# An attention kernel fused with a two-layer softplus network: wide matmuls in the second half of the first layer, and one written order for all steps

## The chip, the cores and the metric

The program runs on one core of a Trainium2 chip. The metric is device time in microseconds (us), lower is better. Before the change three runs took 216.32, 216.36 and 217.01 us, a median of 216.36 us.

## The reference

```python
scores = scale * np.matmul(q, k.transpose(0, 1, 3, 2))      # batch 4, 8 heads, 768 tokens, head size 64
is_global = pos[None, :] < n_global                          # the first 8 tokens of a batch
is_local = (rel >= 0) & (rel < n_local)                      # the last 96 tokens
scores = np.where(is_global | is_local, scores + bias, -1e9) # bias: -slope(head) * distance
a = softmax(scores)
x = matmul(a, v)                                             # as 3072 tokens x 512
h = x @ w_in                                                 # 512 -> 2048
g = np.maximum(h, 0.0) + np.log1p(np.exp(-np.abs(h)))        # softplus
out = g @ w_out                                              # 2048 -> 512
```

Inputs and output are float32. The kernel computes in bfloat16 with float32 sums.

## The kernel before

The 3072 tokens are 24 blocks n of 128; six blocks make one batch of the attention. A block attends to itself, to the block before it, and to the 8 global tokens, which are copied into unused places of the previous block's keys and values. For the two layers the tokens are 12 chunks of 256.

The work is cut into named steps, and each step issues its instructions on several engines. Every engine has its own queue and takes its instructions in the order in which the program writes them; it waits at each for the semaphores that this one needs. The steps:

- `lq lk lv` with a block number: load a block of q, k or v from HBM, with a cast to bfloat16. POOL issues it (line 99). `wi`, `wo`: a quarter of w_in or w_out (lines 105, 110).
- `g` with a number: POOL reads one element of a result of the first layer (line 475), so that what stands behind it in POOL's queue starts no sooner. The numbers are those of `f`.
- `t` (blocks 1 to 7): transpose q and k of a block on the PE and copy them out on DVE, to QT and KT. `d` (from block 8): the same by two DMA transposes that SP issues (lines 251 and 252). `tq tk cq ck` do block 0.
- `s n`: scores. From block 6 on the step s n.0 holds both halves of the heads: matmuls of 64 rows into s_ps, and into s_lo and the bank `o2` for the second half; DVE adds the bias into Z (lines 314, 316, 339). For blocks 0 to 3 the bias comes from matmuls (`z`).
- `e n.half`: exponential on ACT (line 348), four heads.
- `p n.half`: probabilities times v on the PE into x_ps (line 363), one PSUM bank, then on DVE a reciprocal (line 374) and the multiplication into xsf (line 377). xsf is a ring of two blocks, so p of block n writes where block n - 2 lay.
- `x` (blocks 0 to 3, 5) and `y` (all others): transpose xsf into XT, on the PE and DVE, or by one DMA transpose that SP issues (line 388).
- `f`: first layer, 96 steps. A step takes two of the 16 feature blocks of one chunk: for each, four matmuls (512 inputs in four parts) of 256 columns into half of an hT bank (line 416). ACT then does exp and ln(x + 1) on 512 columns (lines 421, 422) into G. hT has two banks.
- `o`: second layer, 96 steps, eight for a chunk: four matmuls of 512 columns (line 438). After four steps a group of 128 tokens is complete; DVE copies it out (line 444) and SP stores it. The banks are `o` and `o2`; from block 6 on until chunk 9 only `o`, since the scores take `o2`. In the last chunk the steps o92 to o95 (line 460) do the last 128 tokens in two parts: o92 and o93 give 320 columns in the bank `o2`, o94 and o95 give 192 columns in the bank `o`.

The first part of the order is written out by hand (ORDER); the rest is sorted by due times: f u at u + 0.5, o u at u + 9.9, attention of block n around 4n - 12.4. The last steps before the change are therefore f95 o86 o87 o88 o89 o90 o91 o92 o93 o94 o95. Gates and loads follow the same times.

Of the kernel before, what the change touches and what calls it, by code (L numbers as in the profile page):

```python
# [19 lines left out]
def kernel(  # L20
# [19 lines left out]
    CT = 2 * P  # L40
# [41 lines left out]
    w_out_c = [const.tile([P, NFB // NWC, DM], BF16, name=f"w_out{c}") for c in range(NWC)]  # L82
# [7 lines left out]
        for n in range(lo, hi):  # L90
            nc.vector.memset(v_t[n][:, :, D : D + 1], 1.0)

    warm_in = const.tile([P, CT], BF16, name="warm_in")
    nc.vector.memset(warm_in[:], 0.0)
    ones(0, 2)

# [24 lines left out]
    def load_v(n):  # L121
# [5 lines left out]
            name=nc.get_next_instruction_name(),  # L127
# [81 lines left out]

    def fill(dst):  # L210

        for _ in range(fillers[0]):
            nc.tensor.matmul(dst, warm_in[:, 0:P], warm_in[:, 0 : dst.shape[1]])
        fillers[0] = 0

    def wide(t):
        return t.rearrange("p a b -> p (a b)")[:, 0:CT]

    def first_of(n):
        return n - n % BPB  # L220

    def qk_bank():
        if fillers[0]:
            fill(ps.tile([P, CT], F32, tag="tr", name="tr_w")[:])
        return ps.tile([P, 2, NPAIR, P], BF16, tag="tr", name="tr")

    def tr_in(tr, j, src):
# [153 lines left out]

    def tr_x(n, by_dma=False):
        xsf, _ = xt.pop(n)
        if n % 2 == 0:
            XT[n // 2] = xtp.tile([P, NPAIR, CT], BF16, tag="XT", name="XT")
        dst = XT[n // 2][:, :, P * (n % 2) : P * (n % 2) + P]
        if by_dma:
            nc.sync.dma_start_transpose(dst, xsf[:].rearrange("p h d -> p (h d)"))
            return
        if n < 2:  # L390
            fillers[0] = 0
            tr = ps2.tile([P, 2, NPAIR, P], BF16, tag="hT", name="tr_x")
# [11 lines left out]
        u = max(u for u in W_IN if 2 * u <= fb)  # L404
        return w_in_c[u], (fb - 2 * u) * P

    def ffn1(c, u):
        if c not in G:
            G[c] = ffn.tile([P, NFB, CT], BF16, tag="G", name="G")
        hT = ps2.tile([P, 2, CT], F32, tag="hT", name="hT")  # L410
        fill(hT[:, 0, :])
        for j in range(2):
            fb = 2 * u + j
            w, fo = w_in_of(fb)
            for m in range(KM):
                nc.tensor.matmul(  # L416
                    hT[:, j, :], w[:, m, fo : fo + P], XT[c][:, m, :],
                    start=(m == 0), stop=(m == KM - 1),
                )
        e_sb = work.tile([P, 2, CT], F32, tag="e_sb", name="e_sb")  # L420
        nc.scalar.activation(e_sb[:], hT[:], AF.Exp)  # L421
        nc.scalar.activation(G[c][:, 2 * u : 2 * u + 2, :], e_sb[:], AF.Ln, bias=1.0)  # L422

    def o_bank(i):
        return o_tile(i, [P, DM])
# [1 line left out]
    def ffn2(c, u):  # L427
        if c == NCH - 1 and u >= NWC:
            ffn2_last(u)
            return  # L430
        ns, kq = divmod(u, NWC)
        if kq == 0:
            O[c, ns] = o_bank(ns if c == 0 or c >= NCH - 3 else 0)
            fill(O[c, ns][:, 0:CT])
        fillers[0] = 0
        o = O[c, ns]
        for a in range(NFB // NWC):
            nc.tensor.matmul(  # L438
                o[:], G[c][:, 4 * kq + a, ns * P : ns * P + P], w_out_c[kq][:, a, :],
                start=(kq == 0 and a == 0), stop=(kq == NWC - 1 and a == 3),  # L440
            )
        if kq == NWC - 1:
            osb = work.tile([P, DM], F32, tag="osb", name="osb")
            nc.vector.tensor_copy(osb[:], O.pop((c, ns))[:])  # L444
            n0 = c * CT + ns * P
            nc.sync.dma_start(out[n0 : n0 + P, :], osb[:])
# [3 lines left out]
    def ffn2_last(u):  # L450

        c, ns = NCH - 1, 1
        c0, w, bank = (0, LW, 1) if u < 6 else (LW, DM - LW, 0)
        fbs = range(NU * (u % 2), NU * (u % 2) + NU)
        if fbs[0] == 0:
            O["last"] = o_bank(bank)
        o = O["last"]
        for fb in fbs:
            kq, a = divmod(fb, NFB // NWC)
            nc.tensor.matmul(  # L460
                o[:, 0:w], G[c][:, fb, ns * P : ns * P + P], w_out_c[kq][:, a, c0 : c0 + w],
                start=(fb == 0), stop=(fb == NFB - 1),
            )
# [7 lines left out]

    def gate(s):

        c, u = divmod(s, NU)
        nc.gpsimd.tensor_copy(gate_t[:], G[c][0:1, 2 * u + 1, 0:1])  # L475

    LAG = 9

    ORDER = """
        w16 lq1 z0.1 lk1 b0 cq0 ck0 tq0 tk0 z0.0 s0.0 e0.0 s0.1 t1 lv0 e0.1 z1.0 b1 z1.1 s1.0 lq2 lk2 lv1  # L480
        s1.1 p0.0 e1.0 e1.1 gk2 lq3 p0.1 t2 p1.0 x0 bb0 lk3 lv2 z2.0 p1.1 gv2 lv3 z2.1 s2.0 s2.1 wi0 wi2 t3
        gk3 e2.0 p2.0 z3.0 s3.0 e2.1 p2.1 lq4 gv3 z3.1 x1 e3.0 s3.1 e3.1 lk4 bb1 p3.0 gk4 x2 lq5 p3.1 f0 x3
        wo0 lk5 gv4 f1 f8 wi4 f2 t4 f9 s4.0 lv4 f10 wo1 wi6 lv5 f11 wo2 s4.1 o4 e4.0 wo3 t5 f3 g11 o0 e4.1
        lq6 gk5 s5.0 f4 p4.0 f12 f5 s5.1 f13 e5.0 o5 o1 lk6 f6 p4.1 f7 gv5 y4 e5.1 lq7 f14 p5.0 f15 o2 p5.1
        lk7 lv6 o6 x5 g7 o3 o7 lk8 t6 lq8 o8 lk9 f16 s6.0 e6.0 f17 f18 t7 p6.0 lv7 g13 lq9 e6.1 f19 s7.0 g15
        lv8 o9 d8 g19 o10 p6.1 gk8 lk10 d9 lq10 y6 o11 e7.0 lk11 f20 g17 e7.1 f21 p7.0 o12 f22 p7.1 s8.0
        e8.0 w2 gv8 o13 o14 y7 o15 e8.1 f23 gk9 p8.0 lv9 s9.0 e9.0 d10 o16 p8.1 e9.1 lq11 d11 gv9 o17 o18
        f24 g23 lk12 p9.0 f25 g21 gk10 y8 f26 p9.1 o19 f27 s10.0 o20 lv10 gk12 lq12 e10.0 f28 y9 o21 gv10
        o22 g27 e10.1 p10.0 g25 f29 gk11 f30 d12 o23 s11.0 lk13 f31 o24 p10.1 lv11 e11.0 lq13 gv11 e11.1 o25
        f32 f33 d13 p11.0 s12.0 e12.0 y10 f34 o26 p11.1 g29 y11 f35 gv12 g31 lk14 lv12 o27 f36 f37 e12.1 o28  # L490
        f38 s13.0 lq14 o29 f39 e13.0 g35 gk14 d14 o30 f40 f41 g33 lk15 lv13 lq15 p12.0 o31 e13.1 g37 f42
        p12.1 g39 lv14 o32 d15 f43 p13.0 s14.0 y12 lq16 g41 lv15 f44 p13.1 g43 lk16 e14.0 o33 y13 gv13 d16
        o34 lk17 gv14 lq17 gk13
    """

    def steady(n):

        s = 4 * n - 12.4
        return {
            f"d{n}": s - 8.2, f"gv{n}": s - 0.95, f"gk{n}": s - 0.9, f"s{n}.0": s,  # L500
            f"e{n}.0": s + 0.7, f"e{n}.1": s + 1.7, f"p{n}.0": s + 1.95, f"p{n}.1": s + 2.95,
            f"y{n}": s + 3.25,
        }

    fillers = [0]

# [28 lines left out]
    def run(name):  # L535
        kind = name.rstrip("0123456789.")
        nums = [int(i) for i in name[len(kind):].split(".")]
        if kind in "fo":
            (ffn1 if kind == "f" else ffn2)(*divmod(nums[0], NU))
        else:  # L540
            KINDS[kind](*nums)

    first_steps = ORDER.split()
    for name in first_steps:
        run(name)
    todo = {}
    for n in range(RV, NB):
        todo.update(steady(n))
    for n in range(RV, NB):
        for names, u in ((f"lq{n}", f"lk{n}"), 4 * n - 25), ((f"lv{n}",), 4 * n - 19):  # L550
            todo[f"g{u}"] = u + 1.6
            for i, name in enumerate(names):
                todo[name] = u + 1.7 + 0.01 * i
    for u in range(NU * NCH):
        todo[f"f{u}"] = u + 0.5
        todo[f"o{u}"] = u + LAG + 0.9
    for name in sorted(todo.keys() - set(first_steps), key=lambda x: (todo[x], x)):
        run(name)


# [33 lines left out]
```

## Time and profile before

The profiled execution took 217.16 us by the device's clock; its span from the first to the last instruction is 215.4 us, so 1.8 us lie around the span. The granted TensorE clock was 1.000 in it.

| engine | busy, us | share of the span | instructions |
|---|---|---|---|
| PE (matmul) | 207.0 | 96% | 2004 |
| PEld (weight load) | 143.5 | 67% | 2004 |
| ACT | 161.4 | 75% | 255 |
| DVE | 109.0 | 51% | 261 |
| POOL | 73.8 | 34% | 115 |

| DMA issued by | what | count | median us from issue to landing |
|---|---|---|---|
| POOL | q, k, v blocks | 70 | 4.6 to 5.1 |
| POOL | w_in, w_out quarters | 8 | 11.6, 13.3 |
| SP | QT, KT, XT transposes | 51 | 4.5 to 4.6 |
| SP | results | 25 | 3.5 (256 KB) |

A matmul's row in the profile lasts until its last result is there; matmuls overlap, so the mean duration of one (273 ns with 256 columns) is longer than the distance at which they follow each other. In the chain of waits a piece "x16" is sixteen matmuls in a row, and its length divided by sixteen is that distance. A name such as `XT<-xsf` says what an instruction writes and reads. SPq and POOLq are the queues that issue DMAs; the bracket at the end of a timeline row tells how long the engine sat idle before it and what ended that.

### The profile page before, as it was taken

Reading aid. Unit: us, or ns where it says so; the run is one execution under the profiler, and the core shown is the slowest. Engines: PE = TensorE matmul, PEld = TensorE weight load, DVE = VectorE, ACT = ScalarE, POOL = GpSimd, SP = SyncE. Lnnn points to the kernel's source line nnn. Section 1 sums busy time; section 2 is a strip of 40 time slices with the busy share of each in tenths; the row PEclk is TensorE's granted clock in tenths of the full one; section 3 lists DMA queues with packets and bytes.
Section 4 is the critical chain, followed back from the end, with each engine's and each line's share of the span. In section 5 each row is a group of like instructions: output and inputs, shape, how many; then the busy total and the mean of one; then the engine's idle time right before and its main releaser. Section 6 shows DMA issues by size and latency. Waiting matters only on the chain.

```text
span 215.4 us, 5027 instructions
## 1 busy us (share of the span) xinstructions
PE 207.0 (96%) x2004; PEld 143.5 (67%) x2004; DVE 109.0 (51%) x261; ACT 161.4 (75%) x255; POOL 73.8 (34%) x115
## 2 busy tenths in 40 slices
PE   8798999999989999999999999999999999999994
PEld 5576777766746677777666666667667667666653
DVE  7485372467457746345755663454664663110121
ACT  4587999929866879889868878878978978777700
POOL 8993663450713235334533333343311000000000
PEclk9999999999999999999999999999999999999999
DMA  9999999999999798999999999999992611201112
GB/s 129 141 161 182 196 198 199 172 181 134 126 140 208 155 113 131 151 108 120 139 194 141 123 125 145 121 156 115 130 148 69 99 29 53 69 3 49 49 49 97
DMA packets 110471, 27.19 MB, mean 126 GB/s; under 512 B 103152, under 2 KB 107504, under 8 KB 110448
## 3 DMA queue, kind: packets, MB, share of 16 engines
q0 software_dynamic: 77024, 13.37, 85.8%
q1 hardware_dynamic: 32384, 13.25, 32.9%
q10 hardware_dynamic: 1040, 0.26, 0.5%
q8 instruction: 15, 0.25, 0.5%
q14 instruction: 8, 0.07, 0.1%
HBM read 27.26 MB, written 6.29 MB: 156 GB/s over the span
## 4 chain that ended last, share of the span: by engine, by line
PE 74%; DMA 17%; POOL 6%; issue 2%; DVE 1%; POOLq 0%; DVEq 0%
PE o L438 32%; PE hT L416 32%; DMA k_t<-in_k_dram 7%; DMA w_in<-in_moe_w_in_dram 6%; DMA XT<-xsf 4%; PE x_ps L363 4%; PE s_ps L277 2%; POOL q_t L99 2%; POOL k_t L99 2%; POOL v_t L99 2%; PE o L460 2%; PE s_lo L277 1%; PE tr L229 0%; DVE xsf L377 0%; POOL w_out L110 0%
## 5 line engine op out<-in xcount | busy, mean ns | idle before, releaser
L416 PE MATMUL hT<-XT,w_in 128*128 128x256 bf16 x768 | 97.7, 273 | 0.5 <-DMA w_in<-in_moe_w_in_dram 0.5
L438 PE MATMUL o<-w_out,G 128*128 128x512 bf16 x368 | 92.3, 379 | 0.0
L416 PEld LDWEIGHTS <-w_in 128*128 128x128 bf16 x768 | 73.9, 98 | 23.7 <-DMA w_in<-in_moe_w_in_dram 0.6
L421 ACT ACTIVATE e_sb<-hT 128x512 f32<-128x512 f32 x96 | 56.4, 588 | 26.1 <-PE hT L416 25.4
L422 ACT ACTIVATE G<-e_sb 128x512 bf16<-128x512 f32 x96 | 60.5, 630 | 3.6
L438 PEld LDWEIGHTS <-G 128*128 128x128 bf16 x368 | 32.7, 98 | 27.3
L348 ACT ACTIVATE Pb<-Z 128x1024 bf16<-128x1024 f32 (+1 forms) x40 | 39.1, 982 | 7.2 <-DVE Z L316 6.9
L444 DVE COPY osb<-o 128x512 f32<-128x512 f32 x23 | 15.9, 692 | 34.0 <-PE o L438 33.9
L316 DVE TENSOR_TENSOR Z<-s_ps,biasA 128x1024 f32<-128x1024 f32 x19 | 23.2, 1223 | 15.9 <-PE s_ps L277 10.7
L475 POOL COPY gate_t<-G 1x1 bf16<-1x1 bf16 x32 | 5.6, 176 | 71.7 <-ACT G L422 71.6
L374 DVE RECIPROCAL rcp<-x_ps 128x4 f32<-128x4 f32 x46 | 8.4, 182 | 36.2 <-PE x_ps L363 36.2
L99 POOL DMA_DIRECT2D v_t<-in_v_dram x24 | 21.5, 898 | 7.3 <-DMA w_in<-in_moe_w_in_dram 3.3
L99 POOL DMA_DIRECT2D k_t<-in_k_dram x23 | 20.4, 888 | 5.6 <-issue 1.9
L99 POOL DMA_DIRECT2D q_t<-in_q_dram x23 | 20.7, 902 | 3.6 <-issue 2.3
L377 DVE TENSOR_TENSOR xsf<-x_ps,rcp 128x256 bf16<-128x256 f32 x46 | 19.5, 424 | 3.9 <-DMA XT<-xsf 2.4
L363 PEld LDWEIGHTS <-Pb 128*128 128x128 bf16 x352 | 16.6, 97 | 5.2 <-ACT Pb L348 1.9
L363 PE MATMUL x_ps<-v_t,Pb 128*128 128x65 bf16 x340 | 18.0, 193 | 2.0 <-ACT Pb L348 1.0
L277 PEld LDWEIGHTS <-KT 64*128 64x128 bf16 x352 | 9.9, 94 | 6.4 <-issue 3.4
L277 PE MATMUL s_ps<-QT,KT 64*128 64x128 bf16 x192 | 9.9, 219 | 1.0 <-DMA KT<-k_t 0.7
L339 DVE TENSOR_TENSOR Z<-s_lo,biasA 128x512 f32<-128x512 f32 x15 | 10.2, 681 | 0.0
L339 DVE TENSOR_TENSOR Z<-o,biasA 128x512 f32<-128x512 f32 x15 | 10.2, 681 | 0.0
L348 ACT ACTIVATE Pb<-s_ps 128x1024 bf16<-128x1024 f32 (+1 forms) x4 | 3.7, 917 | 4.8 <-PE s_ps L277 4.8
(61 smaller groups left out, 95.5 us busy)
## 6 DMA issues: line engine op xcount, KB each, us to landing
out_dram<-osb SPq DMA_DIRECT2D x23, 256.0 KB, 3.5
v_t<-in_v_dram POOLq DMA_DIRECT2D x24, 128.0 KB, 5.1
q_t<-in_q_dram POOLq DMA_DIRECT2D x23, 128.0 KB, 5.0
k_t<-in_k_dram POOLq DMA_DIRECT2D x23, 128.0 KB, 4.6
w_in<-in_moe_w_in_dram POOLq DMA_DIRECT2D x4, 512.0 KB, 11.6
w_out<-in_moe_w_out_dram POOLq DMA_DIRECT2D x4, 512.0 KB, 13.3
XT<-xsf SPq DMA_TRANSPOSE x19, 4.5
k_f<-in_k_dram ACTq DMA_DIRECT2D x1, 256.0 KB, 4.4
```

Source lines behind the costliest of these rows:

```text
L99: nc.gpsimd.dma_start(dst[n][:, :, 0:D], src[b, :, i * P : (i + 1) * P, :].rearrange("h s d -> s h d"))
L277: nc.tensor.matmul(dst(4 * sub + 2 * mm + t), KT[n - t][rows, m, :], QT[n][rows, m, :], start=not pre, stop=not pre or (mm == 1 and (t == ...
L316: nc.vector.tensor_tensor(Z[:], s_ps[:], biasA[:, half, :, :], ALU.add)
L339: nc.vector.tensor_tensor(Z[:, regs, :], s_i[:, 0:4:step, :], bias[:, 1, regs, :], ALU.add)
L348: nc.scalar.activation(Pb[:, 0:nreg, :], src, AF.Exp, scale=inv_sqrt)
L363: nc.tensor.matmul(x_b[:, lh, :], Pb[:, r, :], v_t[n - t][:, h, :], start=(t == 0), stop=(t == 1 or first),)
L377: nc.vector.tensor_tensor(xsf[:, h0 : h0 + 4, :], x_b[:, :, 0:D], rcp[:, h0 : h0 + 4][:, :, None].to_broadcast([P, 4, D]), ALU.mult,)
L416: nc.tensor.matmul(hT[:, j, :], w[:, m, fo : fo + P], XT[c][:, m, :], start=(m == 0), stop=(m == KM - 1),)
L421: nc.scalar.activation(e_sb[:], hT[:], AF.Exp)
L422: nc.scalar.activation(G[c][:, 2 * u : 2 * u + 2, :], e_sb[:], AF.Ln, bias=1.0)
L438: nc.tensor.matmul(o[:], G[c][:, 4 * kq + a, ns * P : ns * P + P], w_out_c[kq][:, a, :], start=(kq == 0 and a == 0), stop=(kq == NWC - 1 a ...
L444: nc.vector.tensor_copy(osb[:], O.pop((c, ns))[:])
```

## The change

The tokens of the two layers are grouped by 512 (g = 0 to 5). XT and G hold a group instead of a chunk; their rings go from 4 to 3 and from 3 to 2 buffers, which are twice as large. For the first three groups (f0 to f47, GC = 6 chunks) a step f is what it was: two feature blocks, 256 columns. From f48 on, token 1536, a step takes one feature block for all 512 tokens: four matmuls of 512 columns instead of eight of 256, into one hT bank; ACT's two instructions keep their size. So f48 now needs four blocks of attention (12 to 15) instead of two. The fillers ahead of the first transposes are 8 matmuls of 512 columns instead of 16 of 256. The due times are gone; the order of all steps is written out. Of the gates, 26 are left of 32.

```diff
-    xtp = ctx.enter_context(tc.tile_pool(name="xtp", bufs=4))
-    ffn = ctx.enter_context(tc.tile_pool(name="ffn", bufs=3))
+    xtp = ctx.enter_context(tc.tile_pool(name="xtp", bufs=3))
+    ffn = ctx.enter_context(tc.tile_pool(name="ffn", bufs=2))
...
-        if n % 2 == 0:
-            XT[n // 2] = xtp.tile([P, NPAIR, CT], BF16, tag="XT", name="XT")
-        dst = XT[n // 2][:, :, P * (n % 2) : P * (n % 2) + P]
+        if n % 4 == 0:
+            XT[n // 4] = xtp.tile([P, NPAIR, 2 * CT], BF16, tag="XT", name="XT")
+        dst = XT[n // 4][:, :, P * (n % 4) : P * (n % 4) + P]
...
+    GC = 6
+
+    def g_half(c):
+        return G[c // 2][:, :, CT * (c % 2) : CT * (c % 2) + CT]
+
+    def ffn1(s):
+
+        g, half = s // NFB, s // NU % 2
+        if g not in G:
+            G[g] = ffn.tile([P, NFB, 2 * CT], BF16, tag="G", name="G")
         hT = ps2.tile([P, 2, CT], F32, tag="hT", name="hT")
-        for j in range(2):
-            fb = 2 * u + j
+        fill(wide(hT[:]))
+        if s < GC * NU:
+            cols = slice(CT * half, CT * half + CT)
+            parts = [(2 * (s % NU) + j, hT[:, j, :]) for j in range(2)]
+            act = G[g][:, 2 * (s % NU) : 2 * (s % NU) + 2, cols]
+        else:
+            cols = slice(0, 2 * CT)
+            parts = [(s % NFB, hT[:].rearrange("p a b -> p (a b)"))]
+            act = G[g][:, s % NFB, :].rearrange("p (a b) -> p a b", a=2)
+        for fb, dst in parts:
             w, fo = w_in_of(fb)
             for m in range(KM):
                 nc.tensor.matmul(
-                    hT[:, j, :], w[:, m, fo : fo + P], XT[c][:, m, :],
+                    dst, w[:, m, fo : fo + P], XT[g][:, m, cols],
                     start=(m == 0), stop=(m == KM - 1),
                 )
...
+        w8 cq0 b0 lq1 ck0 tq0 lk1 lq2 lv0 lk2 b1 z0.1 z0.0 lq3 tk0 s0.0 t1 s0.1 lv1 bb0 e0.0 z1.0 s1.0 p0.0
+        e0.1 z1.1 lk3 lv2 p0.1 lv3 e1.0 wi0 wi2 lk4 lq4 s1.1 t2 e1.1 lq5 z2.0 gk2 p1.0 s2.0 x0 p1.1 z2.1
+        s2.1 e2.0 gv2 gk3 z3.0 lk5 e2.1 wo0 t3 p2.0 wi4 lv4 s3.0 x1 p2.1 z3.1 gv3 e3.0 gk13 s3.1 wi6 e3.1
+        p3.0 bb1 wo1 f0 p3.1 x2 f1 gv4 x3 wo2 f2 lv5 gk4 f8 t4 f9 f10 s4.0 t5 e4.0 wo3 f3 s4.1 e4.1 o0 f11
+        gk5 s5.0 o4 f4 p4.0 f5 p4.1 lk6 f12 s5.1 f6 f13 f14 o5 e5.0 gv5 o1 e5.1 lq6 g6 g12 y4 f7 g9 lq7 o6
+        p5.0 f15 p5.1 lk7 o2 lq8 x5 o7 lv6 lk8 o3 t6 f16 f17 t7 o8 s6.0 e6.0 f18 d8 f19 lq9 lv7 lk9 d9 p6.0
+        e6.1 lk10 o9 s7.0 f20 g15 lq10 gk8 o10 e7.0 p6.1 o11 e7.1 f21 lq11 p7.0 f22 p7.1 y6 s8.0 e8.0 o12
+        gv8 y7 gk9 o13 d10 lv8 o14 o15 e8.1 p8.0 g18 s9.0 lk11 f23 p8.1 o16 y8 o17 lv9 e9.0 lk12 gv9 g21 o18
+        e9.1 f24 lq12 p9.0 lq13 f25 gk10 lv10 f26 p9.1 gv10 f27 s10.0 lk13 g24 d11 lv11 y9 gk11 d12 f28 o19
+        e10.0 f29 lq14 f30 o20 o21 e10.1 p10.0 gk19 s11.0 lk14 g27 lv12 f31 o22 e11.0 d13 f32 d14 p10.1 gv11
+        e11.1 lv13 o23 f33 lk15 lq15 gv12 p11.0 s12.0 e12.0 f34 g30 g31 e12.1 g33 p11.1 o24 y10 y11 lq16 f35
+        p12.0 lk16 lv14 f36 s13.0 e13.0 g35 o25 gk14 d15 lq17 f37 e13.1 p12.1 o26 d16 lk17 y12 g37 o27 p13.0
+        f38 f39 s14.0 o28 gv13 p13.1 e14.0 e14.1 f40 o29 gv14 y13 d17 lv15 gk15 f41 p14.0 s15.0 o30 g39
+        p14.1 e15.0 gv15 gk16 f42 e15.1 o31 lv16 f43 p15.0 y14 s16.0 o32 gk17 lk18 p15.1 gv16 lq18 o33 g43
+        e16.0 f44 o34 y15 e16.1 d18 lq19 g41 o35 lk19 f45 s17.0 lv17 d19 f46 f47 e17.0 e17.1 g47 o36 lq20
+        g45 o37 o38 o39 lv18 gk18 f48 p16.0 f49 s18.0 lk20 gv18 f50 p16.1 f51 gv17 f52 e18.0 d20 o40 e18.1
+        p17.0 f53 y16 g49 s19.0 f54 lv19 o41 f55 e19.0 p17.1 o42 o43 e19.1 g51 p18.0 f56 gk20 f57 p18.1 y17
+        o44 y18 f58 lk21 lq21 g53 p19.0 f59 g57 d21 o45 o46 g55 p19.1 y19 f60 o47 f61 lq22 f62 o48 s20.0
...
+        p23.0 o61 o62 p23.1 f75 f76 y22 y23 o63 f77 f78 o64 f79 o65 o66 o67 f80 f81 o68 f82 f83 o69 f84 o70
+        f85 f86 o71 f87 f88 o76 f89 f90 o72 o77 o73 gv19 f91 o78 o74 f92 o79 f93 o75 o84 f94 o80 o85 f95 o81
+        o82 o83 o86 o87 o88 o89 o90 o92 o93 o91 o94 gk12 o95
```

Steps such as gk12, gk13 and gv19 issue nothing, since those blocks are the first or second of their batch. Scores of blocks 13 to 19 now stand between f36 and f54; the due times had them between f39 and f63.

More of the change, by code (lines that the diff above doesn't have):

```diff
@@ L91, in ones @@
             nc.vector.memset(v_t[n][:, :, D : D + 1], 1.0)
-    warm_in = const.tile([P, CT], BF16, name="warm_in")
+    warm_in = const.tile([P, DM], BF16, name="warm_in")
     nc.vector.memset(warm_in[:], 0.0)
@@ L210, in fill @@
     def fill(dst):
-        for _ in range(fillers[0]):
+        for _ in range(fillers[0] * DM // dst.shape[1]):
             nc.tensor.matmul(dst, warm_in[:, 0:P], warm_in[:, 0 : dst.shape[1]])
@@ L216, in wide @@
     def wide(t):
-        return t.rearrange("p a b -> p (a b)")[:, 0:CT]
+        flat = t.rearrange("p a b -> p (a b)")
+        return flat[:, 0 : min(DM, flat.shape[1] // P * P)]
     def first_of(n):
@@ L223, in qk_bank @@
         if fillers[0]:
-            fill(ps.tile([P, CT], F32, tag="tr", name="tr_w")[:])
+            fill(ps.tile([P, DM], F32, tag="tr", name="tr_w")[:])
         return ps.tile([P, 2, NPAIR, P], BF16, tag="tr", name="tr")
@@ L405, in w_in_of @@
         return w_in_c[u], (fb - 2 * u) * P
-    def ffn1(c, u):
-        if c not in G:
-            G[c] = ffn.tile([P, NFB, CT], BF16, tag="G", name="G")
-        hT = ps2.tile([P, 2, CT], F32, tag="hT", name="hT")
-        fill(hT[:, 0, :])
-        for j in range(2):
-            fb = 2 * u + j
+    GC = 6
[5 more added lines that the diff above has]
+            G[g] = ffn.tile([P, NFB, 2 * CT], BF16, tag="G", name="G")
+        hT = ps2.tile([P, 2, CT], F32, tag="hT", name="hT")
+        fill(wide(hT[:]))
[8 more added lines that the diff above has]
+        for fb, dst in parts:
             w, fo = w_in_of(fb)
@@ L421, in ffn1 @@
         nc.scalar.activation(e_sb[:], hT[:], AF.Exp)
-        nc.scalar.activation(G[c][:, 2 * u : 2 * u + 2, :], e_sb[:], AF.Ln, bias=1.0)
+        nc.scalar.activation(act, e_sb[:], AF.Ln, bias=1.0)
     def o_bank(i):
@@ L433, in ffn2 @@
             O[c, ns] = o_bank(ns if c == 0 or c >= NCH - 3 else 0)
-            fill(O[c, ns][:, 0:CT])
+            fill(O[c, ns][:])
         fillers[0] = 0
@@ L438, in ffn2 @@
             nc.tensor.matmul(
-                o[:], G[c][:, 4 * kq + a, ns * P : ns * P + P], w_out_c[kq][:, a, :],
+                o[:], g_half(c)[:, 4 * kq + a, ns * P : ns * P + P], w_out_c[kq][:, a, :],
                 start=(kq == 0 and a == 0), stop=(kq == NWC - 1 and a == 3),
@@ L460, in ffn2_last @@
             nc.tensor.matmul(
-                o[:, 0:w], G[c][:, fb, ns * P : ns * P + P], w_out_c[kq][:, a, c0 : c0 + w],
+                o[:, 0:w], g_half(c)[:, fb, ns * P : ns * P + P], w_out_c[kq][:, a, c0 : c0 + w],
                 start=(fb == 0), stop=(fb == NFB - 1),
@@ L472, in gate @@
     def gate(s):
-        c, u = divmod(s, NU)
-        nc.gpsimd.tensor_copy(gate_t[:], G[c][0:1, 2 * u + 1, 0:1])
-    LAG = 9
-    ORDER = """
[L480 to L493, printed above, removed]
@@ L494 @@
-    """
[L496 to L503, printed above, removed]
+        if s < GC * NU:
+            last = g_half(s // NU)[0:1, 2 * (s % NU) + 1, 0:1]
+        else:
+            last = G[s // NFB][0:1, s % NFB, 0:1]
+        nc.gpsimd.tensor_copy(gate_t[:], last)
+    ORDER = """
+        w8 cq0 b0 lq1 ck0 tq0 lk1 lq2 lv0 lk2 b1 z0.1 z0.0 lq3 tk0 s0.0 t1 s0.1 lv1 bb0 e0.0 z1.0 s1.0 p0.0
[16 more added lines that the diff above has]
+        o44 y18 f58 lk21 lq21 g53 p19.0 f59 g57 d21 o45 o46 g55 p19.1 y19 f60 o47 f61 lq22 f62 o48 s20.0
+        gv20 f63 o49 o50 gk21 e20.0 lk22 o51 lv20 p20.0 f64 o52 g59 lq23 e20.1 s21.0 lv21 f65 lk23 f66 e21.0
+        d22 o53 o54 e21.1 gk22 p20.1 gv21 f67 f68 d23 o55 g65 g61 p21.0 f69 o56 s22.0 e22.0 lv22 gk23 o57
+        e22.1 o58 p21.1 y20 f70 gv22 f71 p22.0 o59 s23.0 lv23 f72 o60 p22.1 e23.0 gv23 e23.1 f73 y21 f74
+        p23.0 o61 o62 p23.1 f75 f76 y22 y23 o63 f77 f78 o64 f79 o65 o66 o67 f80 f81 o68 f82 f83 o69 f84 o70
+        f85 f86 o71 f87 f88 o76 f89 f90 o72 o77 o73 gv19 f91 o78 o74 f92 o79 f93 o75 o84 f94 o80 o85 f95 o81
+        o82 o83 o86 o87 o88 o89 o90 o92 o93 o91 o94 gk12 o95
@@ L538, in run @@
         if kind in "fo":
-            (ffn1 if kind == "f" else ffn2)(*divmod(nums[0], NU))
+            ffn1(nums[0]) if kind == "f" else ffn2(*divmod(nums[0], NU))
         else:
             KINDS[kind](*nums)
[L543 to L557, printed above, removed]
+    for name in ORDER.split():
         run(name)
```

## The prediction

> **What bounds the kernel now.** I read the page first: PE is busy for 96% of the span at full clock, and the chain that ended last is three quarters PE.
>
> ```profile
> span 215.4 us, 5027 instructions
> PE 207.0 (96%) x2004; PEld 143.5 (67%) x2004; DVE 109.0 (51%) x261; ACT 161.4 (75%) x255; POOL 73.8 (34%) x115
> PE 74%; DMA 17%; POOL 6%; issue 2%; DVE 1%; POOLq 0%; DVEq 0%
> ```
>
> So work that lies beside the PE is worth nothing, and the question is where the PE is not yet full. The chain of waits, taken for 54 to 66 us, shows the last such place: the transpose of block 6 (y6) took 7.93 us to land, DVE could only then write xsf of block 8, and the PE's p8.1 had to wait for x_ps.
>
> ```profile
> 55.60 0.26 PE x_ps L363 x8
> ...
> 56.10 0.39 DVE xsf L377
> 56.49 7.93 DMA XT<-xsf
> ...
> 64.51 0.44 DVE xsf L377
> 64.95 0.04 issue
> 64.99 0.40 PE x_ps L363 x8
> ```
>
> PE's timeline has the two waits there (brackets), and SP's timeline the issues of block 9 (d9) just ahead of y6 at 56.49.
>
> ```profile
> 62.87 0.40 PE L277 MATMUL s_ps<-QT,KT 64*128 64x128 bf16 x8 [0.68 <-DMA KT<-k_t]
> 64.99 0.40 PE L363 MATMUL x_ps<-v_t,Pb 128*128 128x65 bf16 x8 [0.53 <-DVE xsf L377]
> ...
> 53.83 1.19 SPq L251 DMA_TRANSPOSE QT<-q_t  x1
> 55.12 1.27 SPq L252 DMA_TRANSPOSE KT<-k_t  x1
> ```
>
> From 66 us to the last matmul at 212.3 the chain is PE alone. The prices come from there: rows of the chain for a first-layer and a second-layer run, and the timeline of the tail.
>
> ```profile
> 68.43 1.75 PE hT L416 x16
> 103.00 2.59 PE o L438 x12
> ...
> 208.64 3.66 PE L460 MATMUL o<-w_out,G 128*128 128x320 bf16 x32
> 208.84 0.69 DVE L444 COPY osb<-o 128x512 f32<-128x512 f32 x1 [2.76 <-PE o L438]
> 209.56 0.33 SPq L446 DMA_DIRECT2D out_dram<-osb  x1
> ```
>
> **The change part by part.** Sums are made against the profiled execution's 217.16 us (span 215.4); the median of the runs is 216.36, 0.80 less.
>
> *Wide matmuls.* 1.75 / 16 = 109.4 ns for 256 columns, 2.59 / 12 = 215.8 ns for 512. Two narrow ones become one wide one 192 times (48 steps of eight become four). By this row 218.8 - 215.8 = 3.0 ns each, 0.58 us; by the shorter run "0.87 x8" of the same chain 217.5 - 215.8 = 1.7 ns, 0.33 us. I take the middle, -0.45. The halved weight loads give nothing: PEld, 98 ns each, already lies beside the PE. The Trainium skill ("TensorE: Matmul & The Clock Gate", section Back-to-back issue gap) gives N / 2.4 + 2.5 ns, which agrees (109.2 and 215.8); the same section also has a sustained 131 ns for 512 columns. By that figure the saving would be 192 x (218.8 - 131) = 16.9 us; line 438's 512 columns at 215.8 speak against it.
>
> *The start, to t6.* It cannot shorten, because POOL's loads land one behind the other. Ten loads stand ahead of wi0 in both orders, 17 ahead of wi4, 25 ahead of the second load of block 6. They landed at 18.8 (10.66 + 8.1), 29.8 (16.45 + 13.3) and 44.7 (30.31 + 14.4), and f0, f4 and t6 began at 18.85, 30.30 and 44.27, with a wait inside t6. PE's work ahead of each is the same set of steps, but for p3.1 and x2, half a us, which move behind f0. ACT's b1 and bb0 (0.63 + 1.70 us) move ahead of the first exponential, where ACT sat idle 3.68 us. The fillers have the same columns, 16 x 256 = 8 x 512. I take 0; bounds -0.4 (the wait at t6 goes) and +0.4 (wo0 now lands behind lk5, and o0 needs it at once); either is swallowed by the next item.
>
> *From t6 to p8.1.* SP issues d8, d9, y6 in this order in both programs. d9 needs the loads of block 9: q landed last, at 53.8 (44.95 + 8.8), the eighth load behind those of block 6. In the new order k of block 9 is the eighth. So d9 starts at 53.8 again, y6 at 56.4 (p6.1 is now done by 54.5 and no longer matters), and if it takes 7.9 us again p8.1 starts at 65.0 as before. But the PE has then done less: before p8.1 the old order has f16 to f23 and o8 to o16, the new one f16 to f23 and o8 to o15. One step o, 4 x 215.8 = 0.86 us, is still to do: +0.86. The bound below: without any wait the PE is at p8.1 at 44.95 (end of t6) + 8 f (7.0) + 8 o (6.9) + t7 (0.44) + s6 to s9 (0.43 + 3 x 0.65) + five p (1.0) = 62.7, so (62.7 - 64.99) + 0.86 = -1.43. This holds if y6 lands by 62.1, and a transpose after 70 us took 4.7 in the median. The bound above: lk10, lq10, lq11 and lv8 are now issued before d9 and not beside it; if y6 lands 1.5 later, +2.4. I take +0.86, since the row of y6 itself is from this place with the same DMAs in flight.
>
> *From p8.1 to the tail.* The PE was full and keeps the same work, so a gain is excluded beyond the wide matmuls. The attention of blocks 13 to 19 is denser: 17 f, 16 o and 12 e stand from s13.0 to s19.0, where 25 f and 25 o stood. PE: 17 x 0.87 + 16 x 0.86 + 6 x 1.15 = 35.4 us. ACT: 17 x (0.588 + 0.630) + 12 x 0.982 = 32.5 us by the mean rows, still under PE. DVE per block: 1.22 + 2 x 0.68 for Z, 1.2 for two p, 0.5 for gk and gv, 0.5 for copies, 4.8 of 5.9 us. SP per block: two d and a y at 1.25 and some 0.4 for results, 4.1 of 5.9 us, where it was 4.1 of 8.1. POOL has six gates of 0.18 us less. All hide if the transposes land as they did after 70 us (KT 4.2, XT 4.7 in the median): the smallest stretches of PE work between d and its s are 5.5 (block 11), 6.6 (22) and 7.3 us (13), between the last p of a group and its f (48, 64, 80) 8.9 us. I take 0; the bound is priced below. The rings of G and XT are no limit: f64 overwrites what o47 read, which stands four f earlier. The halves of a tile do not wait for each other: x5's copy ran at 42.58 while y4's transpose into the other half of that tile, issued at 38.19, landed 7.0 later.
>
> *The tail.* The order ends o90 o92 o93 o91 o94 o95. o91 is the last step in bank `o`, and o94 starts a new sum in that bank, directly behind it. It must wait for DVE's copy. Before, o92 and o93 covered it: the PE went on at 208.64, the copy of the same group ended at 208.84 + 0.69 = 209.53 and its reader went on at 209.56. So +0.92 us; not under the 0.69 of the copy, not over 1.1 (0.2 more for a semaphore). No other engine has work that the PE could use there, and what follows o95 (copy 0.36, store) is as before.
>
> Sum: 217.16 - 0.45 + 0.86 + 0.92 = 218.49; as a median 217.69, so 217.7.
>
> **The rivals.**
> A, faster: y6 lands early. Its place is y6, its price -2.3 against my sum, and it decides once y6 lands before 62.1; every us earlier than 64.4 gives one. For it: XT transposes took from 2.4 us. Against it: five loads and two transposes in flight, as before. At full it gives 217.7 - 2.3 = 215.4.
> B, the tail does not wait, or hides its wait: 217.7 - 0.9 = 216.8. Against it speaks one bank with one buffer.
> C, slower still: SP becomes the bound in the dense stretch. The KT transposes issued between 48 and 64 us, under the same load by POOL, landed in 6.7 us in the median and 7.7 at most, those after 70 in 4.2. With 1.3 us between the two issues of a d, 7.7 makes 9.0, which misses blocks 11, 22 and 13 by 3.5, 2.4 and 1.7 us. One or two of them missed: 217.7 + 2.5 = 220.2. Against it: in the dense stretch only three loads per 5.9 us are wanted. "DMA: Bandwidth & Descriptors" of the Trainium skill (section Queues, rings and completion order) says that each DMA engine takes turns between the queues that it has work for, packet by packet; 7.93 us for y6 beside 4.5 in the median agree, and by it denser loads cost every transpose.
> D, the wide matmuls of the first layer follow each other faster than those of line 438: each ns of 215.8 that goes is worth 0.19 us, so a chance lies only in many of them. At the 131 ns above it would be 217.7 - 16.4 = 201.3. The 368 wide matmuls of line 438 contradict it.
>
> **How the numbers follow.** A measurement of this kernel tells 0.3% (0.65 us) from no change: under 215.71 is faster, over 217.01 slower. My forecast has 0.47, with a range of its own from 216.9 to 218.6 (0.42 slower, 0.05 same). A has 0.24, between 215.2 and 216.9 (0.14 faster, 0.10 same). B has 0.07 (0.05 same; with A's gain 0.02 faster). C has 0.20, all slower. D has 0.02, faster. Together 0.18 faster, 0.20 same, 0.62 slower. The range for 8 in 10 runs from A's full gain, 215.2, to C, 220.3.
>
> **What would show it.** Right: the chain for 54 to 66 us again has a transpose of XT of 7 us or more that ends at p8.1; line 460 has a wait of about 0.9 us for DVE's copy (line of `osb<-o`) between o91 and o94; line 416 has 576 matmuls, 192 of them with 512 columns at 216 ns. Wrong: p8.1 near 62.7 with no wait (A); idle time of PE's line 277 behind `DMA KT<-k_t` after 66 us (C); line 460 without a wait (B). The forecast falls first with the landing of y6, which is one transfer among ten in flight.

## The result, and the profile after

The changed kernel takes 219.12 us (median of four runs, 218.71 to 219.46) where the kernel before takes 216.34 us beside it: a ratio of 1.0128, 95% interval 1.0103 to 1.0154. It is slower, by 2.8 us and not by the 1.4 us of the forecast. The ratios here and below leave out a run that lies more than 1.5% above the fastest of its kernel; that is one run in all. The profiled execution of after took 219.08 us with a span of 217.2 us, 1.92 us more than that of before (217.16 and 215.4).

The page of after, its span, busy times and the shares of the chain:

```profile
span 217.2 us, 4586 instructions
PE 204.7 (94%) x1778; PEld 123.4 (57%) x1804; DVE 107.0 (49%) x261; ACT 160.7 (74%) x255; POOL 72.6 (33%) x109
PE 73%; DMA 16%; POOL 6%; DVE 2%; issue 2%; SPq 0%; DVEq 0%; POOLq 0%
```

PE still carries the chain, in a longer span. Its busy time can't be set against that of before: 26 of the 1804 matmuls have no record in this trace. The chain of waits of after, taken for 38 to 70 us (start, length, what), has a new link, and the one of before (y6, xsf, x_ps at 64.99) is not in it:

```profile
24.48 18.36 DMA v_t<-in_v_dram
42.84 0.14 issue
42.98 0.40 PE x_ps L364 x8
```

PE's timeline of after shows what that costs, and that p8.1 at 65.42 waits for nothing. (The bracket is the idle time before the row. A matmul's row lasts until its last result, so a wait counted from start to start, as in the table below and in the text on the other kernels, is about 0.2 us longer than its bracket.)

```profile
39.75 1.03 PE L453 MATMUL o<-w_out,G 128*128 128x512 bf16 x4
42.98 0.40 PE L364 MATMUL x_ps<-v_t,Pb 128*128 128x65 bf16 x8 [2.20 <-DMA v_t<-in_v_dram]
...
65.42 0.41 PE L364 MATMUL x_ps<-v_t,Pb 128*128 128x65 bf16 x8
```

The step at 42.98 is p5.0, and what it waits for is lv5, the values of block 5: issued at 24.48, landed at 42.84. Before, lv5 was issued at 23.29 and landed at 36.73, and p5.0 ran at 39.07 without a wait. The landing in the view of v_t at 23.2 to 23.35 us, and PE's timeline, both of before:

```profile
DMA to landing us min/median/max: 13.4/13.4/13.4
...
39.07 0.41 PE L363 MATMUL x_ps<-v_t,Pb 128*128 128x65 bf16 x8
```

SP's timeline of after has y6 two us later than before, behind the second transpose of d9 and a store of results:

```profile
55.55 1.19 SPq L253 DMA_TRANSPOSE KT<-k_t  x1
58.15 0.34 SPq L461 DMA_DIRECT2D out_dram<-osb  x1
58.54 3.00 SPq L389 DMA_TRANSPOSE XT<-xsf  x2
```

It landed at 64.70, 6.2 us after its issue (7.93 before). And the tail of after, the timeline of all engines (one of o91's four matmuls has no record):

```profile
208.65 2.34 PE L475 MATMUL o<-w_out,G 128*128 128x320 bf16 x16
211.04 0.81 PE L453 MATMUL o<-w_out,G 128*128 128x512 bf16 x3
...
211.89 0.69 DVE L459 COPY osb<-o 128x512 f32<-128x512 f32 x1 [0.37 <-PE o L453]
...
212.63 1.48 PE L475 MATMUL o<-w_out,G 128*128 128x192 bf16 x16 [0.78 <-DVE osb L459]
```

o94 starts when the copy of o91's bank is done (211.89 + 0.69 = 212.58).

**Where the 1.92 us are.** From the start of each step in the trace I subtract the PE work that the written order has ahead of it, at the prices of the rows (109 ns for 256 columns, 216 for 512). What is left is the idle time so far; its growth from one step to the next is idle time between them. The prices of the small steps are rough by some tenths, so a single value can even fall (13.64 to 13.38); the difference between the two kernels, which have the same small steps between two lines but for p3.1 and x2, hardly depends on them.

| up to the step | before, us | after, us | difference gained on the way |
|---|---|---|---|
| f0 | 9.88 | 10.70 | +0.82 |
| f16 (just behind t6) | 10.98 | 13.64 | +1.84 |
| p8.1 | 12.09 | 13.38 | -1.37 |
| o91 | 12.85 | 14.12 | -0.02 |
| o95 | 12.91 | 15.13 | +0.95 |

Together +2.22, less 0.40 for the wide matmuls, is 1.82; the last matmul starts at 212.05 before and 213.87 after. In the first line, 0.35 is a later f0 (18.85 and 19.20, each just behind the landing of the first quarter of w_in, 18.80 and 19.15), and the rest is p3.1 and x2, which stand ahead of f0 in the old order and behind it in the new. The value at f0 differs from run to run: over the kernels below it lies between 9.3 and 12.2 us, with a mean of 10.9 in the ten traces with the new start and 10.2 in the eight with the old.

### The profile page after: what moved, and what is told of

The parts are those of the page before. It is cut to its first block, busy times and chain, and to the rows that moved or that the text cites. A ratio compares the mean times of both kernels' runs of the same rounds, so it can differ in the third digit from the quotient of the medians.

```text
span 217.2 us, 4586 instructions
## 1 busy us (share of the span) xinstructions
PE 204.7 (94%) x1778; PEld 123.4 (57%) x1804; DVE 107.0 (49%) x261; ACT 160.7 (74%) x255; POOL 72.6 (33%) x109
## 4 chain that ended last, share of the span: by engine, by line
PE 73%; DMA 16%; POOL 6%; DVE 2%; issue 2%; SPq 0%; DVEq 0%; POOLq 0%
PE o L453 33%; PE hT L431 31%; DMA v_t<-in_v_dram 8%; DMA w_in<-in_moe_w_in_dram 5%; PE x_ps L364 4%; PE s_ps L278 2%; DMA XT<-xsf 2%; PE o L475 2%; POOL v_t L99 2%; PE s_lo L278 1%; POOL q_t L99 1%; POOL k_t L99 1%; POOL w_out L110 1%; POOL w_in L105 1%; DVE osb L459 1%
## 5 line engine op out<-in xcount | busy, mean ns | idle before, releaser
L431 PE MATMUL hT<-XT,w_in 128*128 128x256 bf16 (+1 forms) x567 | 94.4, 307 | 1.7 <-DMA w_in<-in_moe_w_in_dram 1.3
L453 PE MATMUL o<-w_out,G 128*128 128x512 bf16 x351 | 86.4, 379 | 1.3 <-issue 0.5
L431 PEld LDWEIGHTS <-w_in 128*128 128x128 bf16 x576 | 53.5, 98 | 28.2 <-DMA w_in<-in_moe_w_in_dram 1.4
L453 PEld LDWEIGHTS <-G 128*128 128x128 bf16 x368 | 34.4, 98 | 36.8
L349 ACT ACTIVATE Pb<-Z 128x1024 bf16<-128x1024 f32 (+1 forms) x40 | 38.5, 981 | 4.9 <-DVE Z L317 3.5
L317 DVE TENSOR_TENSOR Z<-s_ps,biasA 128x1024 f32<-128x1024 f32 x19 | 23.2, 1220 | 11.2 <-PE s_ps L278 8.6
L493 POOL COPY gate_t<-G 1x1 bf16<-1x1 bf16 x26 | 4.6, 177 | 56.8 <-ACT G L437 56.4
L340 DVE TENSOR_TENSOR Z<-s_lo,biasA 128x512 f32<-128x512 f32 x15 | 10.2, 680 | 0.0
L340 DVE TENSOR_TENSOR Z<-o,biasA 128x512 f32<-128x512 f32 x15 | 10.2, 679 | 0.0
## 6 DMA issues: line engine op xcount, KB each, us to landing
w_in<-in_moe_w_in_dram POOLq DMA_DIRECT2D x4, 512.0 KB, 10.9
```

Source lines behind the costliest of these rows:

```text
L317: nc.vector.tensor_tensor(Z[:], s_ps[:], biasA[:, half, :, :], ALU.add)
L340: nc.vector.tensor_tensor(Z[:, regs, :], s_i[:, 0:4:step, :], bias[:, 1, regs, :], ALU.add)
L349: nc.scalar.activation(Pb[:, 0:nreg, :], src, AF.Exp, scale=inv_sqrt)
L431: nc.tensor.matmul(dst, w[:, m, fo : fo + P], XT[g][:, m, cols], start=(m == 0), stop=(m == KM - 1),)
L453: nc.tensor.matmul(o[:], g_half(c)[:, 4 * kq + a, ns * P : ns * P + P], w_out_c[kq][:, a, :], start=(kq == 0 and a == 0), stop=(kq == NWC ...
```

## The experiments

All ratios are to the kernel before, run on the same chip.

### What makes lv5 late

Three theories: the place of lv5 behind wo2; y4's DMA transpose, which p4.1's earlier place moves from 38.2 to 34.1 us, beside the last weight loads; the wide matmuls and the rest of the order. The first two runs undo one move each in the changed kernel.

**lv5 ahead of wo2.**

```diff
- x3 wo2 f2 lv5 gk4
+ x3 lv5 f2 wo2 gk4
```

> Only the order of two loads is changed back: v of block 5 is issued before the third quarter of w_out, as before the change. Theory Q (the place in POOL's queue made v of block 5 late): it lands before p5.0, the 2.2 us wait of p5.0 goes, and with t6 then waiting for block 6 (landed at 46.4, PE there at 44.8) 0.8 to 2.2 us are gained: 216.9 to 218.3 us. Theory Y (the transpose y4, issued 4 us earlier than before the change, holds up all loads behind it): v of block 5 lands earlier by its place alone, but the third quarter of w_out and block 6 stay late by 2 to 3 us, the wait moves to o6 and t6, and under 1 us is gained: 218.2 to 219.1 us.

1.0144 (1.0113 to 1.0175): no gain, where 0.4 to 1.0% were expected, though lv5 lands at 36.48 and p5.0 does not wait. The time is lost again further on: p8.1 waits 1.1 us for y6, and then p12.1 and p13.0 0.9 and 1.1 us behind y10, in this kernel's chain of waits for 80 to 106 us:

```profile
82.76 6.79 DMA XT<-xsf
...
92.59 0.44 DVE xsf L378
...
93.06 0.40 PE x_ps L364 x8
```

The multiplication of p12 may write xsf only when y10 has read that buffer out of the ring of two, and DVE has the scores of the next block (1.21 + 1.19 us into Z) queued behind it.

**y4 late.** p4.1 moves back from ahead of lk6 to behind o5, and y4, which waits for it, is issued at 38.87.

```diff
- p4.0 f5 p4.1 lk6 f12 ... f14 o5 e5.0 gv5 o1
+ p4.0 f5 lk6 f12 ... f14 o5 p4.1 e5.0 gv5 o1
```

> Only p4.1 is moved back behind o5, so that y4 is issued near 38 us as before the change; the loads keep the new order. Theory Y: v of block 5 lands near 39.5 instead of 42.8, q and k of block 6 near 44.5, the wait of p5.0 goes: 216.7 to 217.2 us. Theory Q: v of block 5 still lands behind the third quarter of w_out, after 42 us, and p5.0 waits as before: 218.8 to 219.4 us.

1.016 (1.0125 to 1.0195). lv5, still behind wo2, lands at 39.54 and p5.0's wait is gone here too. So undoing either move removes it. The time did not follow: f16 waits 0.7 us for y4 itself, which now lands at 45.90, and p8.1 and p14.1 wait 1.1 us each.

Both runs say what delays lv5 and leave open what it costs. The other direction was therefore run: pieces of the new start put into the kernel before, whose later order and narrow matmuls stay.

**The whole new start in the kernel before.** All steps ahead of t6 in the new order.

```diff
- w16 lq1 z0.1 lk1 b0 cq0 ... lk7 lv6 o6 x5 g7 o3 o7 lk8 t6 lq8 o8
+ w16 cq0 b0 lq1 ck0 tq0 ... lk7 o2 lq8 x5 o7 lv6 lk8 o3 g11 g7 t6 o8
```

> The kernel before with nothing changed but the steps ahead of t6, which stand in the new order (two gates, g11 and g7, ahead of t6). If the new start is what delays lv5, p5.0 waits about 2.2 us for it here too; p8.1's old wait for y6 takes up 1.2 to 1.5 of that, and the time is 217.2 to 217.5 us, 1.1 over the kernel before. If the delay of lv5 needs the wide tiles or the later order, no wait at p5.0 and no change: 216.3.

1.0141 (1.0095 to 1.0188), nearly three times what was expected. The wait is there (lv5 lands at 43.12), so it needs neither the wide matmuls nor the later order. But p8.1 takes up nothing of it, as this kernel's chain for 36 to 72 us shows, and SP's timeline:

```profile
24.76 18.36 DMA v_t<-in_v_dram
...
43.26 0.40 PE x_ps L363 x8
...
59.70 7.83 DMA XT<-xsf
...
68.10 0.40 PE x_ps L363 x8
```

```profile
57.08 1.21 SPq L251 DMA_TRANSPOSE QT<-q_t  x1
58.39 1.22 SPq L252 DMA_TRANSPOSE KT<-k_t  x1
59.70 1.31 SPq L388 DMA_TRANSPOSE XT<-xsf  x1
```

y6 is issued 3.2 us later than before (59.70, 56.49) and lands 3.1 us later. SP issues it behind d9, and d9 waited for q of block 9: this load, which stands behind the gate g13, was issued at 47.44 (44.95 before) and landed at 57.02 (53.77 before). So in this trace the lateness reaches y6 through the loads. Idle time up to the last matmul grows from 12.91 to 16.02 us: in this execution the wait at p5.0 arrives whole. (The six runs took 217.7 to 220.9 us; this one took 220.25.)

**The new start with lv5 ahead of wo2, in the kernel before.**

```diff
- x3 wo2 f2 lv5 gk4
+ x3 lv5 f2 wo2 gk4
```

> The kernel before with the new order ahead of t6, and in it lv5 ahead of wo2. If the wait for lv5 is what the new start costs, p5.0 does not wait, no y6 slides, and the time is back at 216.3 to 217.0 us. If the 3.1 us of the new start come from the rest of it too (f0 and t6 later, other loads), it stays above 218.

1.0056 (1.0026 to 1.0086): three fifths of the new start's cost is gone. Its profile has no wait of the PE over 0.4 us from 20 us on. That execution is the fastest of its twelve (216.3 to 219.0 us), so it does not show what the remaining half per cent is. A later f0, as in the table above, is a candidate and not tested.

**One move alone, and both, in the kernel before.**

```diff
- wo1 wi6 lv5 f11 wo2 s4.1            (first move)
+ wo1 wi6 f11 wo2 lv5 s4.1
- f12 f5 s5.1 f13 e5.0 ... f6 p4.1 f7 gv5 y4 e5.1     (second move)
+ f12 f5 p4.1 s5.1 f13 y4 e5.0 ... f6 f7 gv5 e5.1
```

> The kernel before with one step moved: lv5 directly behind wo2. If the place of lv5 is enough, it lands at 41 us or later and p5.0 waits 2 us: 218.3 us. If y4's early transpose is needed too, lv5 lands at 39 to 40 us, directly behind wo2, p5.0 waits at most 0.5 us, and the time is 216.3 to 216.8.

> The kernel before with p4.1 and y4 four steps earlier, so that y4 is issued at about 34 us and not at 38, beside wo2 and wo3. If both parts are needed, wo3 and the loads behind it land 2 to 3 us later than the 41.7 us of before, but lv5 is ahead of them and p5.0 does not wait: 216.3 to 216.8 us. If y4 beside the weights costs by itself (block 6 late, t6 and all behind it), 217.5 or more.

> The kernel before with both moves: lv5 directly behind wo2, and p4.1 and y4 four steps earlier. If the two together are the cause, lv5 lands with y4 at about 42 us instead of 37 to 39, p5.0 waits 2 us, and the time is 218 to 219 us. If other moves of the new start are needed too (loads in another order, t6 later), lv5 lands by 39.5 and the time is 216.3 to 216.8.

lv5 alone: 0.9993 (0.9969 to 1.0016). y4 alone: 1.0001 (0.9973 to 1.0029). Both: 1.0144 (1.0091 to 1.0197). Neither move costs anything; together they cost as much as the whole change. The six runs with both lie apart, two at 217.5 and 217.7 us and four at 220.1 to 221.3; the only profile is of a run of 220.1, so what the two shorter ones wait for isn't shown. PE's timeline of the kernel with both:

```profile
36.28 2.78 PE L416 MATMUL hT<-XT,w_in 128*128 128x256 bf16 x24
42.09 0.62 PE L363 MATMUL x_ps<-v_t,Pb 128*128 128x65 bf16 x8 [3.03 <-DMA v_t<-in_v_dram]
```

and of the one with lv5 alone, where the same step runs at 38.63:

```profile
38.63 0.41 PE L363 MATMUL x_ps<-v_t,Pb 128*128 128x65 bf16 x8
```

The landings show how they meet. With lv5 alone, wo2 lands at 37.62 and lv5 1.0 us behind it. With both, wo2 lands at 38.10 and lv5 4.0 us behind it, at 42.05, while y4 is in flight from 34.12 to 42.71. The transfers of 38 to 42 us by queue (packets, MB, share of the 16 DMA engines; q0 has POOL's loads, q1 SP's transposes), with lv5 alone:

```profile
q0 software_dynamic: 3379, 0.69, 197.9%
```

with both moves:

```profile
q0 software_dynamic: 1620, 0.48, 194.9%
q1 hardware_dynamic: 543, 0.13, 26.3%
```

and in the changed kernel:

```profile
q0 software_dynamic: 1515, 0.51, 179.8%
q1 hardware_dynamic: 544, 0.13, 29.6%
```

Where the transpose moves its 0.13 MB, the loads move 0.18 to 0.21 MB less, in just the 4 us in which lv5 is the next load to land. The Trainium skill ("DMA: Bandwidth & Descriptors", section Queues, rings and completion order) has each DMA engine take turns between its queues packet by packet; the shares above agree with it. Why the one small load is held until about the transpose's end, with wo3 only 1.9 us behind it, is not settled.

### What the later order costs by itself

**The old start in the changed kernel.** The steps ahead of t6 as before (lq8 directly behind t6); all else changed.

```diff
- w8 cq0 b0 lq1 ck0 tq0 ... lk7 o2 lq8 x5 o7 lv6 lk8 o3 t6 f16
+ w8 lq1 z0.1 lk1 b0 cq0 ... lk7 lv6 o6 x5 g7 o3 o7 lk8 t6 lq8 f16
```

> The changed kernel with nothing undone but the steps ahead of t6, which stand in the order of the kernel before (lq8 directly behind t6). If the start was the one step of the prediction that failed, p5.0 does not wait, p8.1 waits for y6 until 65 us with one step o less done, the tail waits 0.95 us, and the time is that of the forecast, 1.4 over the kernel before: 217.7 us. If the lateness is handed on to y10 as when lv5 alone was moved, p12.1 and p13.0 wait 1 us each and it stays at 219.

1.0121 (1.0086 to 1.0156): the expectation for one failed step was wrong. PE's timeline of this kernel, in its longest run (220.93 us; the other five took 218.0 to 219.8, so the waits of most are smaller):

```profile
59.97 0.40 PE L278 MATMUL s_ps<-QT,KT 64*128 64x128 bf16 x8 [1.47 <-DMA KT<-k_t]
...
94.26 0.40 PE L364 MATMUL x_ps<-v_t,Pb 128*128 128x65 bf16 x8 [0.94 <-DVE xsf L378]
...
214.26 1.48 PE L475 MATMUL o<-w_out,G 128*128 128x192 bf16 x16 [0.78 <-DVE osb L459]
```

s8.0 waits for the keys of block 8 (issued at 53.08, landed at 59.92), p13.0 behind y10 (6.4 us in flight), o94 for the copy. In the changed kernel the keys of block 8 land at 59.58 and s8.0 starts at 59.64: the PE, late from p5.0, meets them without a wait. So the start costs 3.1 us alone, and all the rest of the change 2.6 alone, and the two together cost no more. That the one's lateness covers the other's is how these two traces read; other executions were not profiled.

**A ring of four for xsf**, in the changed kernel and in the kernel before:

```diff
- work.tile([P, H, D], BF16, tag="xsf", name="xsf"),
+ work4.tile([P, H, D], BF16, tag="xsf", name="xsf"),
```

> Only the ring of xsf gets four buffers instead of two, so that p of block n need not wait until y of block n-2 has landed; the loads keep the new order. Theory R (the slow XT transposes reach the PE through this ring alone): the waits of DVE for XT and with them those of p8.1 and p12 to p15 go, but the wait of p5.0 for v of block 5 stays: 0.3 to 0.8 us are gained, 218.3 to 218.8 us. Rival S (it is SP's queue and the DMA engines; the transposes of keys land late as well and the scores wait next): no change, 219.1 us.

> The kernel before, with a ring of four for xsf and nothing else. Theory R: its wait of p8.1 for y6 (0.69 us) goes, that of s9.0 for KT (0.84 us) stays: 0.5 to 0.9 us faster than before, 215.0 to 215.4 us. Rival S: no change.

In the changed kernel 1.0115 (1.0076 to 1.0154), with p5.0's wait of 2.0 us still there; in the kernel before 0.9985 (0.9961 to 1.0009), not to be told from no change. The expectation of theory R, 0.5 to 0.9 us for the kernel before, was not met.

**Without the loads of v for blocks 11 to 16**, on top of lv5 ahead of wo2. Their p uses what the buffers held, so a part of the attention isn't computed.

> As e1 (v of block 5 early), but the loads of v of blocks 11 to 16 are left out; their p reads what lay in the buffer, so this part of the attention is not computed. If POOL's loads slow SP's transposes by sharing the DMA engines, y10 and y11, which took 6.8 and 6.3 us in e1 between 82 and 92 us, take 5 us or less, and the waits of p12.1 and p13.0 (0.87 and 1.10 us) go: 217.2 us. If the transposes are slow by themselves or for each other, they take 6 to 7 us again: 219.3 us.

One run, 218.25 us. p12.1 and p13.0 no longer wait; y10 takes 4.3 us where it took 6.8 with those loads. This alone shows little: with all those loads in the program y10 also took 4.0 us (y4 late) and 5.1 us (the changed kernel). The traces of before and after say it better. The transposes of XT during which no packet of POOL's loads (q0) moved took 2.4 to 2.5 us before the change (y9, y22, y23) and 2.4 to 3.0 after it (seven of 19). The others took 3.7 to 7.9 us before, but for one of 2.5, and 4.3 to 8.4 after. So a transpose beside loads took longer. In the stretch in question, y8 to y13 took 2.5 to 6.0 us before and 4.3 to 6.5 after; that the denser order does this is likely and not tested.

### The tail and the wide matmuls

**o91 first.**

```diff
- o90 o92 o93 o91 o94 gk12 o95
+ o90 o91 o92 o93 o94 gk12 o95
```

> Only the tail is changed back: o91 before o92 and o93, so that DVE's copy of the bank is covered by them. My prediction's step: 0.92 us are gained, 218.2 us. The rival, that the wait is hidden or that the end is set by the stores: no gain, 219.1 us.

The wait is gone: idle time from o91 to o95 is 0.06 us, and 1.0 in the changed kernel. The ratio is 1.0136 (1.0102 to 1.017) all the same, though its interval is too wide to exclude a gain of 0.9 us (0.4%); the profiled execution waited 2.1 us at p5.0 and 1.2 and 1.1 at p12.1 and p13.0, where the changed kernel's did not wait at the last two.

**All matmuls narrow** (`GC = 12`, so no step has 512 tokens).

> Only the wide matmuls are undone: all steps f take two feature blocks of 256 columns, in the same order of steps (GC = 12). My prediction's price: 192 wide matmuls become 384 narrow ones at 1.7 to 3.0 ns a pair, so 0.33 to 0.58 us slower: 219.5 to 219.7 us. The rival, that wide matmuls cost something beside the PE (the exponential can begin only when a whole bank is there, the weights come at half the rate): no change or faster, 218.6 to 219.1 us.

1.0191 (1.0161 to 1.022), 0.3 to 0.6% above the three kernels that ran beside it (1.0136 to 1.016). The intervals touch, so a gain of the wide matmuls of 0.7 to 1.2 us is likely but not shown; that they cost something is not borne out. Its profile is worth a second look: the same start, but f0 1.4 us later, so that y4 is issued at 35.48 and not at 34.09. There lv5 lands at 39.09, 1.0 behind wo2, and p5.0 does not wait. From 38 to 42 us the queues move the same 0.48 and 0.13 MB as with both moves; but the transpose's first packet comes after 39.4 us, behind lv5's landing. As these traces read, what counts is which of the two comes first, and here 1.4 us decided it.

### All waits taken away

lv5 ahead of wo2, the ring of four and o91 first together; then the whole old start in place of lv5's move; then also o19 ahead of f24, which in the trace of the first of these had waited 0.66 us for y7 (in that of the second it does not).

> The three suspected waits together are taken away: v of block 5 before the third quarter of w_out, the ring of xsf with four buffers, o91 before o92. Theory R: the lateness that the PE gathers from f0 to the end falls from 4.4 us to about 1 us, and the wide matmuls save 0.4 us: 214.0 to 215.0 us, faster than the kernel before (215.9 in the last comparison). Rival S: the next thing that waits for the DMAs takes the place, only the 0.95 us of the tail is gained for sure: 217.3 to 218.3 us.

> The changed kernel with the steps ahead of t6 in the order of the kernel before (lq8 directly behind t6), xsf in a ring of four, and o91 ahead of o92. If the new order of the start costs something beyond the wait for lv5 (f0 began 0.5 to 1 us later than in the kernel before in most profiles), this gives 216.1 us, 0.7 under the version with lv5 ahead of wo2; if f0's start only varies from run to run, 216.8 again.

> The first kernel of this set (old start, ring of four, o91 first) with o19 ahead of f24. f24 waited 0.66 us for y7 at 66.5 us; o19 (0.86 us) needs only f23. If that wait is what is left between this order and a faster one, 0.6 us less: 215.5. If the us is handed on to the next transposes (y8 to y11), the same as without it.

1.0004 (0.9979 to 1.0029), 1.0023 (0.9997 to 1.0049) and 1.0008 (0.9987 to 1.003). That removes the whole loss, which none of the first version's three edits did alone in the changed kernel, and no version beats the kernel before: the 214.0 to 215.0 us of theory R were not met. In the profile of the second, idle time from f0 to o95 is 1.58 us where it is 3.03 before, yet its runs are no faster; what the other executions wait for is not shown.

## Why the prediction was right and wrong

The direction was right (slower, 62%), and 219.1 lies in the range; the size was half.

*The start, to t6: this step failed.* It took 0, with bounds of 0.4 on either side. The two profiled executions differ by +1.84 there, from f0 to f16, and by +0.82 ahead of f0, where the text saw that half a us moves behind f0 and counted it as nothing. The runs with nothing but lv5 and y4 moved put the price of these two moves at 1.44%, 3.1 us. It looked at the loads that f0, f4 and t6 wait for and counted how many stand ahead of each. lv5 has nearly the same number ahead of it in both orders (only wo2 passed it), and was not looked at, since p5.0 did not wait in the trace of before. Its slack there was 39.07 - 36.73 = 2.3 us. In the kernel before, wo2 ahead of it uses 1.9 us of that (landing at 38.59), and y4's earlier issue, which was not priced, the rest and 3.0 us more (42.05). The sentence that either bound "is swallowed by the next item" failed as well: with the new start alone y6 slid too and p8.1 passed all 3.1 us on. Undoing the start alone does not bring the time back, though (1.0121): a second term at nothing, below, stands behind it. (t6 began at 44.10, not at 44.27; nothing hangs on it.)

*From t6 to p8.1: +0.86 taken, -1.37 measured, near the lower bound of -1.43.* d9's second transpose was issued at 55.55 (55.12 before), as argued, but y6 not at 56.4: ahead of it in SP's queue stands the store of the group that o11 completes, and with the PE late DVE had copied that group only at 58.12, so y6 went out at 58.54. (That p6.1 had held y6 before the change was a misreading: the row at 55.60 is p7.0. p6.1 ran at 52.70, and y6 went out behind d9, 55.12 + 1.27.) It then took 6.2 us, and the late PE did not have to wait. In the two traces both items together are thus +0.47 against +0.86, close by luck: the lateness of p5.0 stands in the place of the step o that was to be still undone at p8.1. With p5.0's wait undone the pin is back: idle time up to p8.1 is 12.11 us with lv5 ahead of wo2, 12.09 before. In the kernels with the order of before it varies: PE's idle time at s9.0 and p8.1, by the brackets, was 0.68 and 0.53 us in the trace that the prediction read, none and 0.99 with lv5 alone moved, and none at either with y4 alone. It was a draw of that execution and not a fixed price.

*From p8.1 to the tail: 0 taken, -0.02 measured*, but, as the traces read, only because the PE was late. With the start undone 1.3 us of waits appear at p12.1 and p13.0. This second term at nothing was therefore too low as well. Its mechanism is that of rival C, slow transposes beside loads, at another place: not the scores behind KT, but xsf's ring of two behind XT, which the text did not follow.

*The tail: +0.92 taken, +0.95 measured* in the trace. *Wide matmuls: -0.45 taken.* The -0.40 above follows from the rounded prices. The groups of after by form show the mean time until a matmul's result is there, and nine of the 192 wide ones have no record. Start to start they stand 109 and 216 ns apart (eight wide ones take 1.73 us in the chain of after):

```profile
L431 PE MATMUL hT<-XT,w_in 128*128 128x256 bf16 x384 | 48.2, 273 | 1.3 <-DMA w_in<-in_moe_w_in_dram 1.3
L431 PE MATMUL hT<-XT,w_in 128*128 128x512 bf16 x183 | 46.2, 379 | 0.4
```

That ends rival D. A did not happen, since y6 landed at 64.70 and not by 62.1, nor did B, since o94 waited. C's own sign, a wait behind the transposes of keys after 66 us, isn't there: between p5.0 and o94 no wait of the PE in this trace is over 0.3 us.

*The step to the median.* The sum was 218.49 for a profiled execution and measured 219.08, 0.59 more. The text then took off 0.80 because the profiled execution of before was that far above its median. The one of after lies on its median. So more than half of the miss, 0.84 of 1.43 us, is this subtraction, which took for granted that an execution of after under the profiler would lie as far above its median as that of before.

## What to carry to other kernels

When an order of loads changes, give every load its slack (need minus landing) and price whatever shares the DMA engines with it in its last microseconds, other queues too; a wait that is absent from the trace may be 2 us away. Test moves in pairs as well as alone: two harmless moves cost 3 us together, and the two halves of this change cost no more together than either one. A wait seen in one execution that hangs on a transfer among many is a range and not a term of a sum.

## What the hardware showed

- A DMA transpose of 128 KB, issued at 34.1 us behind queued loads, moved nothing in its first 4 us (queue q1 has no packet before 38 us) and then all in the next 4, in which POOL's loads moved about 0.5 MB, against 0.69 without it. With nothing else moving (y22 and y23 of before) the first packet came 1.2 us after the issue.
- A 128 KB load of v lands 1.0 us behind the weight quarter ahead of it, or 3.0 to 4.0 us behind it when such a transpose is at work.
- The same transpose (XT) took 2.4 to 3.0 us when no packet of POOL's loads moved during it, and 3.7 to 8.4 us otherwise, with one exception of 2.5 (38 transposes of the traces of before and after).
- A sum into a bank that DVE has yet to copy out waits 0.95 us beyond the matmul before it, 0.69 of it the copy.
